# Gated mix of a spectral filter and a dense layer: the row transform in 32 half-width units, begun during the first matmul stage

## The chip, the cores and the metric

The kernel runs on one core of a Trainium2 chip. The metric is the device time of one execution in microseconds (us). Three runs of the kernel before gave 1273.38, 1273.94 and 1275.4 us; the median is 1273.94. The engines are named as in the profile: PE (TensorE, matrix products), PEld (its weight loads), DVE (VectorE), ACT (ScalarE), POOL (GpSimd) and SP (SyncE, which only issues transfers here). Each engine carries out its own instructions strictly in their order. ACT, POOL and SP also issue DMAs; such a line of the profile has a "q" behind the engine's name.

## The reference

For an input x of 2048 rows and 1024 columns, two branches are mixed by a gate for each row, and all gradients are taken for a given grad_out. It comes to nine outputs.

```python
def _A_ref(x, w_r, w_i):                    # spectral branch
    X = jnp.fft.rfft2(x.astype(jnp.float32), axes=(-2, -1))   # 2048 x 513, complex
    X = X * (w_r + 1j * w_i)
    return jnp.fft.irfft2(X, s=(S, D), axes=(-2, -1)).astype(jnp.bfloat16)

def _B_ref(x, w1, b1, w2, b2):              # dense branch, hidden width F = 3584
    h = jnp.einsum("bsd,df->bsf", x, w1) + b1
    r = jnp.where(h > 0, h, 0)
    return jnp.einsum("bsf,fd->bsd", r * r, w2) + b2

g = _sigmoid((x * gate_w).sum(-1, keepdims=True))
out = g * _A_ref(x, w_r, w_i) + (1 - g) * _B_ref(x, w1, b1, w2, b2)
# outputs: out, and its gradients for x, w_r, w_i, w1, b1, w2, b2, gate_w
```

The gradient of the spectral branch needs the same transform of the gated grad_out, so everything spectral is done for two arrays, called T = 0 (x) and T = 1 (the gradient).

## The kernel before, in words

**Two streams.** The main stream is the dense branch, in four stages one after another, all on TensorE in bf16:

- `mlp_in` (L671, 11 to 446 us): 112 units for the hidden layer (ph, L683) and 112 for its gradient (pd, L693), each of 8 matmuls of 128x512. A pair of them, 3.45 us, is counted as one unit here. ACT makes rT and h2T from ph, DVE makes dhT from pd, and both results go to DRAM. ph and pd share two banks of PSUM (the matmul accumulator memory). The weights w1g come in groups by SP, three buffers deep.
- `mlp_grads` (L785, 446 to 883 us): the gradients of w2 (pw, L824) and of w1 (pw, L840), 112 units of 16 matmuls, some 3.6 us each, into two banks. ACT evicts each unit (wo, L828 and L845). The left operand grp comes from DRAM by transposing DMAs on SP, two tiles in turn.
- `mlp_out` (L867, 883 to 1094 us; acc, L914), and then the gradient of x (`GradOfX.products`, 1094 to 1265 us; L1023).

The side stream is the spectral branch, as matmuls with small matrices of cosines and sines:

- The *first stages* (`first_stage_of_x`, `first_stage_of_grad`, L635 and L649) take 16 tiles for each T along the columns: fold (DVE), matmuls pk (L261), ACT copy ft, matmuls pu (`column_stage`, L294), copies and sums into u, store into the DRAM scratch z_scr by POOL (L283).
- `fft_mid` (L302) is the row transform. It runs over m = 0 to 15; each m covers a pair of row groups (n = 0, 1), 512 columns wide and for both T. For each m: load z (four DMAs) and the filter rows wn, sums pm (DVE), matmuls px with the matrices am (L378), ACT copies x (L380), products with the filter (DVE, L386 and L388), y (L395, L396), matmuls pv with bm (L414), ACT copy vc (L419), sums pc (DVE, L421 and L422), stores to y_scr (POOL, L438). The gradients of the filter are gs (DVE) and gw (ACT, L455, with buffers of two), stored by four DMAs (L461).
- The spectrum has 513 columns. Column 512 (the Nyquist column) and column 0 come by a way of their own: `edges` (L334) loads the edge columns of z_scr by nine small DMAs on SP into ed, low and mid, `edges_through` (L346) multiplies them with am (32 matmuls sp of 4 columns, L357) into ex, and DVE puts ex into columns 0 and 512 of x. On the way back, DVE gathers column 512 of y into ye, 32 matmuls si (L427) transform it, and DVE writes the outcome into column 0 of pc.
- `fft_out` (L506) takes 32 tiles. For each: load r from y_scr, issued by ACT (L521), DVE sums rf (L529, L530), matmuls pki (L537) on r and rf, ACT copy rt (L539), matmuls pui (L294), copies and sums, store to ax_scr. With the T = 0 tiles SP loads w2 in seven transfers of 1 MB.

**What sets the order.** Both streams are generators. `spread(main, side, per_main)` (L1146) runs main units and draws `per_main` side steps for each of them; the order that results, with the scheduler's own view of when operands are there, is the order of every engine. Before the change, in mlp_in 0.9 steps are drawn for a step of the main stream (72 of them, counted from where the transposes of the inputs are over), then the rest of the first stages follows at once, and beside the last units only the sums of the rows of dbn (the gradient of b2) run. `fft_mid` and half of `fft_out` are spread evenly over mlp_grads, some 1.6 steps for a unit; the other half of `fft_out` lies in mlp_out. The side stream has two 2-bank PSUM tiles in turn (tag "ps2"); small tiles (tag "tr") have a pool of their own, `tps`.

Of the kernel before, what the change touches and what calls it, by code (L numbers as in the profile page):

```python
# [10 lines left out]
P = 128  # L11
# [39 lines left out]
def build_consts(g: Geo):  # L51
# [54 lines left out]
    am, bm = np.zeros((P, R1 // 2, 2, P)), np.zeros((P, R1 // 2, 2, P))  # L106
    for m in range(R1 // 2):
        for n, k in enumerate(pair_of(m, R1)):
# [3 lines left out]
            bm[:, m, n] = np.block([[C_.T, S_.T], [-S_.T, C_.T]])  # L112
    c["am"] = (am * XS).astype(FDT_NP)
    c["bm"] = bm.astype(FDT_NP)
# [21 lines left out]
def kernel(  # L136
# [76 lines left out]
    z_scr = dram.tile([R1, R2, 2, 2, H], FDT, name="z_scr")  # L213
    y_scr = dram.tile([R1, R2, 2, 2, H], FDT, name="y_scr")
    rows_of = lambda scr, T: scr[:][:, :, :, T, :].rearrange("c (p i) x l -> i (c p) x l", i=S2)
# [52 lines left out]
    def first_columns(fb, cf, T, i, ft, earlier=None):  # L268
# [6 lines left out]
        uv = u[:].rearrange("p (c g i) -> p c g i", c=2, g=4)  # L275
        even = pu[:, 0, :].rearrange("p (h c i) -> p c h i", h=2, c=2)
        nc.scalar.copy(out=uv[:, 0, 0::2, :], in_=even[:, 0])
        nc.scalar.mul(out=uv[:, 1, 0::2, :], in_=even[:, 1], mul=flip[:])  # L278

        X, Y = (w[:, :, x] for x in range(2))  # L280
        V(out=uv[:, :, 1::2, 0 : P // 2], in0=X, in1=Y, op=ALU.add)
        V(out=uv[:, :, 3::-2, P - 1 : P // 2 - 1 : -1], in0=X, in1=Y, op=ALU.subtract)
        st(out=rows_of(z_scr, T)[i], in_=u[:].rearrange("p (x l) -> p x l", x=2))  # L283
# [18 lines left out]
    def fft_mid():  # L302
        fb, fbs = pool("f2", "right")
        NM, G = R1 // 2, nc.gpsimd
        lanes = [slice(R2 * n, R2 * (n + 1)) for n in range(2)]
        every = lambda w_, k: w_.rearrange("(q k) l -> k q l", k=R1)[k]
        am = fb.tile([P, NM, 2, P], FDT, name="am", tag="am")
        ld(out=am[:], in_=cten["am"].ap())
        bm = fb.tile([P, NM, 2, P], FDT, name="bm", tag="bm")
        ld(out=bm[:], in_=cten["bm"].ap())  # L310

        def inputs(m):
            z = fb.tile([P, 2, 2, H], FDT, name="z", tag="z", bufs=2)
            for n, c in enumerate((m, R1 // 2 + m)):
                for x in range(2):
                    ld(out=z[lanes[x], n], in_=z_scr[:][c, :, x ^ n if m else x])
            wn = fb.tile([P, 2, LW], BF16, name="wn", tag="wn", bufs=2)
            for c_, src_w in enumerate((A_w_r, A_w_i)):
                for n, k in enumerate(pair_of(m, R1)):
                    ld(out=wn[lanes[n], c_, 0:W1], in_=every(src_w, k))  # L320
            return z, wn
# [146 lines left out]
        for _ in range(3):  # L468
            yield
# [853 lines left out]
```

## Time and profile before

| what | value |
|---|---|
| median of three runs | 1273.94 us (1273.38 to 1275.4) |
| the profiled execution | 1274.6 us |
| its span, first to last instruction | 1272.8 us |
| mean granted clock of TensorE | 0.999 |
| busy in the span: PE, DVE, ACT, POOL | 1249.1, 706.4, 503.7, 270.9 us |
| instructions of PE, DVE, ACT, POOL in the trace | 6753, 1602, 793, 424 |
| moved by DMA | 233.27 MB, 183 GB/s in the mean |

The busy time of an engine is the time in which the profile shows it at work; issuing a DMA is not counted. The "40 slices" cut the span into 40 equal parts and give the busy share of each in tenths. A line of the groups names line, engine, operation, output and inputs with their sizes, the number of instructions, then busy time and the mean of one in ns, then idle time before them and what ended it. A line of the timeline has start, duration, engine, line, operation, output and inputs, and in brackets the idle time before it and what it waited for. A line of the waits has the total in us, the number of times and the longest.

### The profile page before, as it was taken

To read this page: it belongs to the slowest core of one execution; us is meant where nothing else is said; L and a number is where in the kernel's file an instruction comes from. 1 tells how busy PE (TensorE), PEld (TensorE's weight loads), DVE (VectorE), ACT (ScalarE), POOL (GpSimd) and SP (SyncE) were. 2 spreads that over 40 slices of the span, in tenths; PEclk is the share of its full clock that TensorE was granted. 3 is DMA by queue.
4 is the path that set the end of the run, shared out by engine and by line. 5 is a ranking of instruction groups with operands and counts; after the bars stand their busy time and mean duration, and the time that the engine had idled before them with its cause. 6 is when DMAs were issued, how large, how long until landed. Compare 5 with 4: busy or idle time off the path is not lost.

```text
span 1272.8 us, 18282 instructions
## 1 busy us (share of the span) xinstructions
PE 1249.1 (98%) x6753; PEld 609.6 (48%) x6884; DVE 706.4 (56%) x1602; ACT 503.7 (40%) x793; POOL 270.9 (21%) x424
## 2 busy tenths in 40 slices
PE   8999999999999999999999999999999999999997
PEld 5555544555544444444444444555445454444443
DVE  3554433445481216676756661343867767896573
ACT  4656654666633334554555552443112111010100
POOL 0111111111110124445545542222010101000000
PEclk9999999999999999999999999999999999999999
DMA  9566353646353879998898678994999898565530
GB/s 287 199 186 186 134 157 117 182 140 183 112 153 70 196 194 201 259 244 193 194 193 201 133 161 230 305 244 164 229 225 221 192 212 203 153 190 174 169 113 34
DMA packets 326260, 233.27 MB, mean 183 GB/s; under 512 B 195308, under 2 KB 279434, under 8 KB 325914
## 3 DMA queue, kind: packets, MB, share of 16 engines
q1 hardware_dynamic: 291120, 141.19, 48.4%
q0 software_dynamic: 26144, 82.47, 19.1%
q10 hardware_dynamic: 8906, 8.43, 2.3%
q8 instruction: 54, 0.88, 0.3%
q14 instruction: 36, 0.29, 0.1%
HBM read 106.19 MB, written 81.81 MB: 148 GB/s over the span
## 4 chain that ended last, share of the span: by engine, by line
PE 61%; DVE 4%; DMA 2%; issue 2%; ACT 1%; POOL 0%; SPq 0%; ACTq 0%; DVEq 0%; POOLq 0%
PE acc L914 14%; PE pw L824 13%; PE pw L840 12%; PE xX L1023 7%; PE xV L1023 3%; PE pd L693 3%; PE ph L683 3%; PE xZ L1023 2%; PE pui L294 1%; PE pki L537 1%; PE px L378 1%; PE pv L414 1%; DMA r<-y_scr 1%; DMA out_dram<-wo 1%; ACT x L380 1%
## 5 line engine op out<-in xcount | busy, mean ns | idle before, releaser
L683 PE MATMUL ph<-xT,w1g 128*128 128x512 bf16 x864 | 216.9, 379 | 2.7 <-DMA w1g<-in_B_w_dram 1.2
L693 PE MATMUL pd<-dbT,w2T 128*128 128x512 bf16 x877 | 209.8, 379 | 1.6 <-DVE dhT L697 0.4
L840 PE MATMUL pw<-grp,res 128*128 128x512 bf16 x872 | 198.8, 379 | 2.3 <-ACT wo L845 1.1
L824 PE MATMUL pw<-dbn,grp 128*128 128x512 bf16 x876 | 198.9, 379 | 1.9 <-ACT wo L828 0.7
L914 PE MATMUL acc<-w,hblk 128*128 128x512 bf16 x873 | 196.5, 379 | 1.2
L697 DVE SCALAR_TENSOR_TENSOR dhT<-pd,rT 128x512 bf16<-128x512 f32 x112 | 77.3, 691 | 202.9 <-PE pd L693 159.7
L824 PEld LDWEIGHTS <-grp 128*128 128x128 bf16 x896 | 87.0, 98 | 104.6 <-issue 1.5
L693 PEld LDWEIGHTS <-w2T 128*128 128x128 bf16 x896 | 87.0, 98 | 103.5 <-issue 1.2
L840 PEld LDWEIGHTS <-res 128*128 128x128 bf16 x896 | 86.1, 98 | 99.8 <-issue 1.4
L914 PEld LDWEIGHTS <-hblk 128*128 128x128 bf16 x896 | 86.4, 98 | 97.9
L683 PEld LDWEIGHTS <-w1g 128*128 128x128 bf16 x896 | 84.5, 98 | 90.5 <-DMA w1g<-in_B_w_dram 1.5
L685 ACT ACTIVATE rT<-ph,b1col 128x512 bf16<-128x512 f32 x112 | 77.0, 687 | 116.7 <-PE ph L683 113.1
L982 ACT ACTIVATE g<-gatew_bc,dsc 128x1024 f32<-128x1024 bf16 x16 | 18.3, 1148 | 146.8 <-DVE gxo L1032 120.6
L845 ACT CAST wo<-pw 128x512 bf16<-128x512 f32 x56 | 32.6, 585 | 106.3 <-PE pw L840 57.1
L686 ACT ACTIVATE h2T<-rT 128x512 bf16<-128x512 bf16 x112 | 70.5, 630 | 2.5
L539 ACT CAST rt<-pki 128x1024 f16<-128x1024 f32 x32 | 32.5, 1015 | 95.0 <-PE pki L537 92.9
L1023 PEld LDWEIGHTS <-dS 128*128 128x128 f16 x448 | 43.7, 98 | 53.3 <-DVE dS L1011 0.5
L828 ACT CAST wo<-pw 128x512 bf16<-128x512 f32 x56 | 32.6, 583 | 87.5 <-PE pw L824 58.6
L380 ACT CAST x<-px 64x1024 f16<-64x1024 f32 x64 | 64.4, 1007 | 0.7
L283 POOL DMA_DIRECT2D z_scr<-u x32 | 23.2, 726 | 171.2 <-ACT u L278 101.4
L738 POOL DMA_DIRECT2D h2T_scr<-h2T x28 | 20.4, 727 | 183.0 <-ACT h2T L686 167.4
L566 POOL DMA_DIRECT2D ax_scr<-yo x32 | 17.3, 540 | 167.9 <-DVE yo L565 126.2
(189 smaller groups left out, 1610.6 us busy)
## 6 DMA issues: line engine op xcount, KB each, us to landing
h2T_scr<-h2T POOLq DMA_DIRECT2D x28, 512.0 KB, 4.3
dhT_scr<-dhT POOLq DMA_DIRECT2D x28, 512.0 KB, 4.6
hblk<-h2T_scr SPq DMA_DIRECT2D x16, 896.0 KB, 7.6
hblk<-dhT_scr SPq DMA_DIRECT2D x16, 896.0 KB, 8.7
z_scr<-u POOLq DMA_DIRECT2D x32, 256.0 KB, 3.1
z<-z_scr SPq DMA_DIRECT2D x64, 128.0 KB, 3.5
y_scr<-pc POOLq DMA_DIRECT2D x64, 128.0 KB, 4.3
r<-y_scr ACTq DMA_DIRECT2D x32, 256.0 KB, 4.3
```

The costliest lines, as they stand in the source:

```text
L380: nc.scalar.copy(out=x[lanes[n], c, :, 0:H], in_=px[lanes[c]])
L683: mm(ph[:], lhsT=w1g[:, dc, fc % 2 * P : (fc % 2 + 1) * P], rhs=xT[:, dc, ss], start=(dc == 0), stop=(dc == DC - 1))
L685: nc.scalar.activation(rT[:], ph[:], ACT.Relu, bias=b1col[:, fc : fc + 1])
L686: nc.scalar.activation(h2T, rT[:], ACT.Square)
L693: mm(pd[:], lhsT=w_[:, ec, fc % FGC * P : (fc % FGC + 1) * P], rhs=dbT[:, ec, ss], start=(ec == 0), stop=(ec == DC - 1),)
L697: return STT(out=dhT, in0=pd[:], scalar=2.0, in1=rT[:], op0=ALU.mult, op1=ALU.mult, accum_out=gb1part[:, fc, sb : sb + 1],)
L824: mm(pw[:], lhsT=cur[:, t, fb_ * P : (fb_ + 1) * P], rhs=dbn[:, t, hf * H : (hf + 1) * H], start=(t == 0), stop=(t == NT - 1),)
L828: last = nc.scalar.copy(out=wo[:, hf * H : (hf + 1) * H], in_=pw[:])
L840: mm(pw[:], lhsT=xr[t][:, d_ * P : (d_ + 1) * P], rhs=cur[:, t, :], start=(t == 0), stop=(t == NT - 1),)
L845: nc.scalar.copy(out=wo[:], in_=pw[:])
L914: turn["PE"] = mm(acc[:], lhsT=cur[:, fc, t2 * P : (t2 + 1) * P], rhs=w2[:, fc, cs], start=(fc == 0), stop=(fc == FC - 1))
L1023: mm(acc[:], lhsT=lhs[:, fc, :], rhs=rhs[:, fc, :], start=start and fc == 0, stop=fc == KH - 1, skip_group_check=True,)
```

## The change

`fft_mid` is done in 32 units instead of 16: for each m first the upper half of the columns (h = 1), then the lower (h = 0), each 256 wide. All tiles of a unit (z, pm, x, t, y, pc, gs) have half the width, and both n and both T of a unit go through one PSUM tile. The scratch arrays z_scr and y_scr get the layout (row group, row, real/imaginary, h, T, column), so that a z load or a y store of a unit is one DMA for each n; a row tile (the u stores, by POOL; the r loads, by ACT) now takes three DMAs instead of one. In fft_out ACT copies the even columns of r into a tile re, from which the matmuls read.

The Nyquist column is packed: its filtered value (eh, from the h = 1 unit) is added to or subtracted from column 0 of the products in the h = 0 unit. The si matmuls, ye and the repairs of pc disappear. For this the rows of the matrices are interleaved anew (ab, one load of 128 KB for each m, in place of am and bm); am is loaded in two halves for the edges alone, into a buffer of the products. The edge columns take twelve DMAs instead of nine. gs, gw and pm have one buffer instead of two; gw is written in two halves and stored once for each m. ACT instead of DVE puts ex into x.

The side stream is one generator (first stages, sums of db, fft_mid, fft_out), drawn at 1.25 steps for a unit through all of mlp_in. 9 of the 32 units of fft_mid begin there, the others run beside mlp_grads. fft_out keeps its place to within two units, and mlp_out and the gradient of x keep their order. When the transposes of the inputs are over, `tps` is closed and ph/pd get four banks instead of two; sp and other small tiles move to "ps2". To make room, w1g has two buffers instead of three, the tiles h2T and dhT three instead of four, and of the two tiles for grp one lies in a pool opened with mlp_grads.

```diff
+    def rows_of(issue, scr, T, i, sb, stored):
+        far = scr[:].rearrange("c (p i) x h t l -> i t (c p) x h l", i=S2)[i, T]
+        near = sb[:].rearrange("p (x h l) -> p x h l", x=2, h=2)
+        lo, hi = slice(0, P // 2), slice(P // 2, P)
+        pairs = [(far[lo], near[lo])] + [(far[hi][:, 1 - x], near[hi][:, x]) for x in range(2)]
+        for a, b in pairs:
+            issue(out=a, in_=b) if stored else issue(out=b, in_=a)
...
+        def edges():
...
+            for x in range(2):
+                for t in range(2):
+                    e = 2 * x + t
+                    ld(out=ed[lanes[0], :, 0, e], in_=col[:, 0:NM, x, t])
+                    ld(out=low[lanes[1], :, e], in_=col[:, NM:, 1 - x, t])
+                    ld(out=mid[lanes[0], e : e + 1], in_=col[:, NM, 1 - x, t : t + 1])
...
+            sp = fps.tile([P, NM, 2, 4], FP32, name="sp", tag="ps2", bufs=2)
+            for h in range(2):
...
+                if h == 0:
+                    am = some_am(1)
+                    for _ in range(4):
+                        yield
...
+        def transform(m, h, pm, ex):
+            x = fb.tile([P, 2, 2, WL], FDT, name="x", tag="x", bufs=2)
+            px = fps.tile([P, 2, 2, HW], FP32, name="px", tag="ps2", bufs=2)
+            for n in range(2):
+                mm(px[:, n], lhsT=mats[m][:, 0, n, :], rhs=pm[:, n], start=True, stop=True)
+            for n in range(2):
+                for c in range(2):
+                    nc.scalar.copy(out=x[lanes[n], c, :, 0:HW], in_=px[lanes[c], n])
+            nc.scalar.copy(out=x[:, :, :, h * HW], in_=ex[:, m, :, :, h])
+            return x
...
+        def back(m, h, y):
...
+            for n in (1, 0):
+                mm(pv[:, n], lhsT=mats[m][:, 1, n, :], rhs=y[:, n], start=True, stop=True)
...
+                vc = fb.tile([P, 2, HW], FP32, name="vc", tag="vc")
+                nc.scalar.copy(out=vc[:], in_=pv[:, 1])
+                V(out=pc[:, 0], in0=pv[:, 0], in1=vc[:], op=ALU.add)
+                V(out=pc[:, 1], in0=pv[:, 0], in1=vc[:], op=ALU.subtract)
+            for n, c in enumerate((m, R1 // 2 + m)):
+                st(out=y_scr[:][c, :, :, h].rearrange("r x t l -> (r x) t l"), in_=pc[:, n])
...
+        def grads_out(m, h, gs, gw):
+            nc.scalar.mul(
+                out=gw[:, :, h * HW : (h + 1) * HW].rearrange("p c (i g) -> p c i g", g=4),
+                in_=gs[:, :, 0:HW].rearrange("p c (g i) -> p c i g", g=4), mul=GS,
+            )
+            nc.scalar.mul(out=gw[:, :, h * H], in_=gs[:, :, h * HW], mul=0.5 * GS)
+            if h == 0:
...
+        turns = [(m, h) for m in range(NM) for h in (1, 0)]
...
+        for u, (m, h) in enumerate(turns):
+            if h:
+                eh = fb.tile([P, 2, 2, 2], FDT, name="eh", tag="eh")
+            x = transform(m, h, pm, ex)
             yield
             if held:
+                back(*turns[u - 1], held)
+            tt = products(h, x, w)
+            yield
+            if u:
+                grads_out(*turns[u - 1], gs, gw)
+            held = joined(h, tt, eh)
+            yield
+            gs = grads_of_w(h, x)
...
     def fft_out():
...
-            nc.scalar.dma_start(out=r[n][:].rearrange("p (x l) -> p x l", x=2), in_=rows_of(y_scr, T)[i])
+            rows_of(nc.scalar.dma_start, y_scr, T, i, r[n], False)
...
+            evens[n] = fb.tile([P, 2, 2, P], FDT, name="re", tag="re", bufs=2)
+            for im in range(2):
+                nc.scalar.copy(
+                    out=evens[n][:, im].rearrange("p g (h i) -> p g h i", h=2),
+                    in_=rv[:, im, :, 0::2, :].rearrange("p h g i -> p g h i"),
+                )
...
     def mlp_in():
+        banks, drawn = [mps], [0]
+
+        def bank(name):
+            drawn[0] += 1
+            return banks[drawn[0] // 2 % len(banks)].tile([P, SW], FP32, name=name, tag="ph", bufs=2)
+
+        def more_banks():
+            tps_s.close()
+            more, mores = pool("mps1b", "left", PSUM)
+            banks.append(more)
+            mpss.callback(mores.close)
...
-            w1[fp] = wb.tile([P, DC, PW], BF16, name="w1g", tag="w1g", bufs=3)
+            w1[fp] = wb.tile([P, DC, PW], BF16, name="w1g", tag="w1g", bufs=2)
...
-    first = firsts()
-    n = 0
-    mixed = spread(units, first, 0.9)
-    while n < 72:
-        next(mixed)
-        n += 1
-    for _ in first:
-        pass
...
+    def aside():
         yield from stage
         yield from first_stage_of_grad()
...
+        yield from sums_of_db()
         yield from fft_mid()
         yield from fft_out()
 
...
+    for _ in spread(units, spec, 1.25):
+        pass
+    grads = mlp_grads()
     next(grads), next(grads)
-    todo = 13 + 6 * (R1 // 2) + 2 * NT
+    todo = 22 + 2 * (NT + 4) + NT + 1 + 9 + 4 * R1 + 1 + 4 + 2 * NT - count[0]
     for _ in spread(grads, spec, todo / (2.0 * FG * FGC * NH - 2)):
         pass
```

## The prediction, made before the changed kernel was run

> **What bounds the kernel now.** I read four views in this order: the busy times, the 40 slices, the waits of TensorE, and then windows of 40 us, because the question is only where TensorE is not full. The page first:
>
> ```profile
> PE 1249.1 (98%) x6753; PEld 609.6 (48%) x6884; DVE 706.4 (56%) x1602; ACT 503.7 (40%) x793; POOL 270.9 (21%) x424
> ...
> PE   8999999999999999999999999999999999999997
> ...
> ACT  4656654666633334554555552443112111010100
> ...
> PEclk9999999999999999999999999999999999999999
> ```
>
> TensorE is busy for 98% of the span, in every slice but the first and the last, at an undisturbed clock. So engine time elsewhere is free as long as it makes TensorE wait for nothing, and a change can win only what matmuls it removes and what idle time it closes. How much idle time there is inside is read from the windows (length, then busy time of PE, weight load, DVE, ACT, POOL, clock, DMA share, GB/s):
>
> ```profile
> 320.00:360.00 40.00, 39.73 (x228) 20.15 (x232) 21.24 (x55) 24.02 (x46) 5.81 (x8) 1.00 0.49 133
> 360.00:400.00 40.00, 39.42 (x179) 17.77 (x182) 22.88 (x37) 14.55 (x23) 4.36 (x6) 1.00 0.25 92
> ...
> 480.00:520.00 40.00, 39.79 (x184) 18.17 (x187) 25.91 (x46) 20.17 (x23) 18.32 (x26) 1.00 1.04 216
> ...
> 600.00:640.00 40.00, 39.15 (x184) 17.89 (x186) 25.23 (x45) 23.06 (x25) 20.11 (x31) 1.00 0.95 180
> 640.00:680.00 40.00, 38.90 (x181) 17.66 (x184) 25.51 (x47) 21.37 (x24) 18.77 (x29) 1.00 1.02 213
> 680.00:720.00 40.00, 39.20 (x183) 17.89 (x186) 27.49 (x47) 20.31 (x24) 21.60 (x33) 1.00 0.63 151
> ...
> 760.00:800.00 40.00, 38.55 (x204) 18.29 (x207) 11.82 (x35) 11.67 (x19) 12.80 (x24) 1.00 0.91 238
> ```
>
> A full window shows 39.79. Against it the row transform (fft_mid, 450 to 770 us) loses 0.64 + 0.89 + 0.59 = 2.1 us in three windows, its passage into fft_out 1.24 us, and the passage from the first stages to the sums of db 0.37 us (360 to 400). The idle time is really a little longer than shown: an isolated 512-column matmul is written down as 379 ns, while in a row of them one starts every 216 ns, so each stop hides 0.16 us. With that I count 2.8, 2.0 and 0.8 us. That is nearly all the change can touch. The waits and one place in the timeline tell what kind they are:
>
> ```profile
> PE pw L840 <- ACT wo L845: 1.1, 2, 0.6
> PE pv L414 <- ACT x L380: 0.9, 2, 0.6
> PE pw L824 <- ACT wo L828: 0.7, 1, 0.7
> ```
>
> ```profile
> 630.76 2.00 ACT L455 ACTIVATE gw<-gs 128x1024 bf16<-128x1024 f16 x1 [4.39 <-DVE gs L454]
> 632.40 0.19 PE L427 MATMUL si<-ye,bm 128*128 128x4 f16 x2
> 632.67 1.05 ACT L828 CAST wo<-pw 128x512 bf16<-128x512 f32 x2
> 633.29 3.61 PE L824 MATMUL pw<-dbn,grp 128*128 128x512 bf16 x16 [0.69 <-ACT wo L828]
> ```
>
> The eviction wo, which frees a bank for the next 3.6 us of matmuls, stood behind one 2.0 us ScalarE instruction (gw), and TensorE stopped. Long instructions on ScalarE's in-order queue are the cause inside fft_mid.
>
> **The change part by part.** The sum is made against the profiled execution: 1272.8 us of span and 1.8 us around it, 1274.6, which is 0.66 above the median of the runs shown, 1273.94.
>
> *Matmuls removed.* The 32 si matmuls go. They are listed at 166 ns, but the 32 sp matmuls (same shape) ran back to back in 0.95 us. I take 32 x 0.03 = 0.9 us gained; the other end is 16 pairs at the 0.19 us shown, 3.1. All other matmuls keep their columns, only split differently.
>
> *Pieces half as long.* px copies go from 64x1024 at 1.007 us to 64x512 (the 128x512 wo costs 0.59), gw from one of 1.98 us per m to two of about half, vc (1.02) and the pc sums (1.22) likewise. The queue ahead of wo gets shorter, and a unit of half the work comes every 3.25 main units (12 us; 24 us per m) where a whole m came every 4.6 (17 us). The three windows' idle time can go wholly; I take all 2.8 us, ends 0 and 2.8. What is late next at such a place is wo itself, 0.59 us after pw, which two banks cover.
>
> *Four banks and continuous side work in mlp_in.* The side stream (first stages, sums of db, then 9 of the 32 fft_mid units) runs at 1.25 steps per main unit to the end of mlp_in, where before it ran at 0.9 and then only sums. The ph/pd tiles get four banks instead of two, so the stop at 371 us (0.8 with the hidden part) should be covered: 0.8 gained, ends 0 and 0.8. Against it, the denser first stages put a pu block after its own pk with five 0.216 us matmuls between, 1.08 us, where the copy ft takes 1.01: a few stops of 0.1 to 0.2 us, +0.3 (0 to 3).
>
> *Edges.* In the changed order the first sp matmul is unit 83 of 112. The loads of its edge columns stand on SP behind the w1g load, whose buffer is now one of two and comes free when unit 79 ends. That leaves about 3.5 units at 3.45 us, 12.1 us. Behind it SP issues w1g, am and twelve edge loads:
>
> ```profile
> 457.57 0.63 SPq L341 DMA_DIRECT2D ed<-z_scr  x1
> ...
> 466.67 0.67 SPq L343 DMA_DIRECT2D mid<-z_scr  x1
> 470.06 0.16 DVE L348 COPY ed<-mid 64x4 f16<-64x4 f16 x1
> ...
> 478.58 0.95 PE L357 MATMUL sp<-ed,am 128*128 128x4 f16 x32
> ```
>
> One issue is 0.63 to 0.67 us and the last one lands 3.4 us later. 0.9 + 12 x 0.65 + 3.4 + 1 for the DVE pieces is 13.1; up to 16 if the issues meet as many gaps as the nine here (9.1 us from first to last). So TensorE waits 1 to 4 us, unless the scheduler's place for w1g lets SP start earlier; I take +1.5, ends 0 and 4. Queued behind that wait are the ph/pd units, nothing else hides it. The second half of am is loaded over the first and has three units, 10 us, against the 5.5 in which the whole am landed: nothing.
>
> *Second grp tile.* It now lies in memory that mlp_in gives up, so its four transposes (3.4 to 3.9 us each on SP, 6.4 to landing) start at the end of mlp_in: 22 us against the 8 units of the first group, 29 us. Nothing; with 7 us less cover it would be late.
>
> *Passage to fft_out.* The chain is shorter: half a vc, pc at 0.69 instead of 1.22, two y_scr stores instead of four, no si. But an r tile is now three DMAs, and all are issued by ScalarE, ahead of wo:
>
> ```profile
> 778.77 0.97 ACTq L521 DMA_DIRECT2D r<-y_scr  x2
> 779.86 0.59 ACT L845 CAST wo<-pw 128x512 bf16<-128x512 f32 x1 [6.11 <-DMA out_dram<-wo]
> 780.50 3.61 PE L840 MATMUL pw<-grp,res 128*128 128x512 bf16 x15 [0.51 <-ACT wo L845]
> 784.45 0.29 DVE L529 TENSOR_TENSOR rf<-r 128x256 f16<-128x256 f16 x1 [12.03 <-DMA r<-y_scr]
> ```
>
> Six issues of 0.37 us instead of two are +1.5; shorter chain -1.9. New is that ScalarE itself copies the even columns (re<-r) and so waits for r, where only DVE and TensorE waited before. I take -0.4 (-1.9 to +5.4, worked out under the rivals).
>
> *Hidden work.* ScalarE gets some 290 more instructions: 64 re copies (0.42 us, by the DVE copy of that size), 64 more issues (23 us), 32 ex copies, each px copy's fixed part; about 55 us. In 450 to 760 us it is busy 155 of 310 us and in 80 to 350 us 164 of 270, so it is covered. POOL's 64 more z_scr issues (0.53 to 0.73 us) come on 271 of 1273 us, SP's 19 instructions on an idle queue, DVE's pieces at 56%. Single gs, gw and pm buffers: a gw store lands in 4.0 us in the median, one m lasts 24 us; +0.3 (0 to 4, for a chain gs, gw, store that runs late beside 1 MB loads). If that cover went, ScalarE would hold back wo and the price would be the excess over one unit, 3.6 us.
>
> One rule speaks against the split. The Trainium skill, "DMA: Bandwidth & Descriptors", "Anatomy of one DMA", puts a fixed part of about 2.0 us on each DMA, and by it 128 more transfers would be 256 us of latency, ruinous if any were in series. This case's trace agrees on the size: 64 KB gw stores land in 4.0 us, 256 KB r loads in 4.3. They overlap here, so my sum holds only the issue times. By the rule alone the passage would cost two more fixed parts, 4 us, and the forecast would be no change.
>
> A second one is "Double-buffer for performance" in "Trainium Kernel Development and Optimization", "Best Practices", which the single gw and gs buffers go against. No row of before shows them single.
>
> *Sum:* -0.9 - 2.8 - 0.8 + 0.3 + 1.5 - 0.4 + 0.3 = -2.8. 1274.6 becomes 1271.8 in a profiled run, 1271.1 in the median.
>
> **The rivals.** 0.2%, 2.55 us, is about what a measurement here tells from no change.
>
> *No change.* The edge wait at 4 us and a stop or two of fft_mid surviving (half of 2.8 gained): -0.9 - 1.4 - 0.8 + 0.3 + 4 - 0.4 + 0.3 = +1.1, so 1275.0; with only one of them, 1272.5 to 1273.6. For it speaks the SP arithmetic above; against it, the w1g load may be issued earlier.
>
> *Slower: ScalarE caught at the passage.* It stands in order: r issues that wait until y_scr has landed, wo, re copies that wait until r has landed, wo. An r load landed 4.8 to 9.6 us after its issue beside the seven 1 MB w2 loads (12.7 us in the median). At 9.6, ScalarE is held about 9.6 - 1.5 - 0.6 = 7.5 us, of which one unit of pw covers 3.6: 3.9 us of idle TensorE, with the 1.5 of issues +5.4 instead of -0.4. That gives +3.0, 1276.9, and a second such tile 1280.8. It decides from about 9 us of landing on. Against it: the third tile's load was already 4 us ahead in the trace, and later ones longer.
>
> *The stops don't go.* If they come from DMA landing and not from long ScalarE pieces, only si and the bank gain remain: 1273.9. The line at 630.76 speaks against it; this goes with no change.
>
> **How the numbers follow.** Forecast 0.44 (faster 0.40, same 0.04, as 1271.1 lies near the bound of 1271.4); no change 0.25; ScalarE caught 0.31 (slower, 0.01 of it same). The range goes from 1266.0 (si at 3.1, passage -1.9, no edge wait: -8.6 at most, little chance below) to 1281.0, two caught tiles. The forecast's own range is 1267.0 to 1273.0. Sum of the cases: faster 0.40, same 0.30, slower 0.30.
>
> **What would show it.** Right: 32 matmuls fewer than 6753; the windows between 480 and 760 us at 39.6 to 39.8; PE waits for wo gone; a wait of sp for an ed copy near unit 83 (370 to 390 us) of 1 to 2 us. The passage, around 770 to 790 us, decides: a re copy that waits for r with wo behind it and PE pw waiting for wo is the slower rival. Wrong in another way: waits of PE for ft or u in 60 to 350 us (the denser first stages), or ScalarE waiting for gw's store.

## The result, and the profile after

The changed kernel takes 1304.09 us (median; 1302.24 to 1305.32) against 1274.67 for the kernel before beside it: a ratio of 1.023, 95% interval 1.0212 to 1.0248. It is slower by 29 us, where the forecast had been 1271.1 and the range ended at 1281. The profiled execution took 1302.24 us with a span of 1300.5.

The page of the changed kernel, the busy times, TensorE's slices and the granted clock:

```profile
span 1300.5 us, 18819 instructions
...
PE 1259.0 (97%) x6722; PEld 610.4 (47%) x6852; DVE 719.4 (55%) x1742; ACT 536.6 (41%) x1016; POOL 313.8 (24%) x520
...
PE   9999999999899979999999998899999999999998
...
PEclk9999999999999989999999998899999999999999
```

Two things differ from before. TensorE has weak slices around 340, 470 and 780 to 845 us, and the clock row is lower in the last two of these places; the windows below show it lower in the first and around 660 us too. Of the 27.7 us by which the span grew, 17.8 are more idle time (41.5 against 23.7) and 9.9 are more busy time, although 32 matmuls are gone (the weight loads, of which every one is recorded, fell from 6884 to 6852). The end of the kernel hides a part of the loss. The last instruction of VectorE, before and after, is

```profile
1265.11 0.69 DVE L1032 TENSOR_TENSOR gxo<-xV,g 128x512 bf16<-128x512 f32 x1 [2.33 <-PE xV L1023]
```

```profile
1295.76 0.69 DVE L1064 TENSOR_TENSOR gxo<-xV,g 128x512 bf16<-128x512 f32 x1 [2.33 <-PE xV L1055]
```

so the work ends 30.7 us later, and the rest of the span behind it (the last store and the closing instructions, called the tail below) is 4.0 us instead of 7.0. The windows in which the time is lost (columns as before):

```profile
320.00:360.00 40.00, 35.61 (x172) 16.05 (x174) 7.46 (x27) 13.16 (x20) 8.05 (x12) 0.96 0.55 138
440.00:480.00 40.00, 32.32 (x144) 14.21 (x146) 25.04 (x66) 22.49 (x42) 15.79 (x26) 0.96 0.72 165
640.00:680.00 40.00, 37.72 (x166) 16.72 (x167) 20.31 (x48) 17.44 (x35) 15.42 (x25) 0.96 0.70 151
760.00:800.00 40.00, 36.10 (x163) 16.21 (x165) 9.55 (x23) 11.05 (x21) 9.69 (x18) 0.96 0.66 176
800.00:840.00 40.00, 33.89 (x183) 16.74 (x187) 10.17 (x43) 17.11 (x34) 6.49 (x12) 0.87 1.07 275
```

No engine is near full in them, so it is not work that was too much but waits. (The DMA share is over 1 in the last window, but it was 1.13 in the same window of the kernel before, with TensorE full.) The waits of TensorE, and of ScalarE before gw:

```profile
PE pw L871 <- ACT wo L876: 9.5, 3, 3.9
PE pw L855 <- ACT wo L859: 8.6, 3, 6.0
PE sp L355 <- DVE ed L350: 4.1, 1, 4.1
PE pd L724 <- DVE dhT L728: 1.7, 3, 0.9
```

```profile
ACT gw L466 <- DMA out_dram<-gw: 25.7, 4, 8.2
```

A few long stops make up nearly all of it. Each has a place in the timeline. First the edges:

```profile
334.54 0.37 SPq L746 DMA_DIRECT2D w1g<-in_B_w_dram  x1
...
337.32 2.92 SPq L334 DMA_DIRECT2D mid<-z_scr  x1
...
350.66 0.68 PE L355 MATMUL sp<-ed,am 128*128 128x4 f16 x16 [4.07 <-DVE ed L350]
```

SP issued w1g at 334.5, needed 13 us for am and the twelve edge loads (one tiny mid load held it 2.9 us), and TensorE stood 4.1 us before sp. Then gw:

```profile
469.08 1.09 POOL L474 DMA_DIRECT2D out_dram<-gw  x2
...
478.36 1.06 ACT L466 ACTIVATE gw<-gs 128x512 bf16<-128x512 f16 x1 [8.16 <-DMA out_dram<-gw]
...
479.43 1.05 ACT L859 CAST wo<-pw 128x512 bf16<-128x512 f32 x2
480.04 1.44 PE L855 MATMUL pw<-dbn,grp 128*128 128x512 bf16 x3 [6.00 <-ACT wo L859]
...
481.70 4.65 PE L855 MATMUL pw<-dbn,grp 128*128 128x512 bf16 x16 [0.22 <-issue]
```

With one gw buffer the next gw waits until the four stores of the last have landed, 8.2 us, and the two evictions wo stand behind it on ScalarE. The last line is the slow clock: 16 matmuls take 4.65 us instead of 3.61 after the stop, the later ones at full speed again. And the passage to fft_out:

```profile
788.45 4.14 ACTq L227 DMA_DIRECT2D r<-y_scr  x6
...
792.70 0.58 ACT L876 CAST wo<-pw 128x512 bf16<-128x512 f32 x1 [8.47 <-DMA r<-y_scr]
793.34 5.30 PE L871 MATMUL pw<-grp,res 128*128 128x512 bf16 x15 [2.82 <-ACT wo L876]
...
800.93 0.40 ACT L542 COPY re<-r 128x256 f16<-128x256 f16 x1 [2.95 <-DMA r<-y_scr]
...
801.87 8.42 PE L871 MATMUL pw<-grp,res 128*128 128x512 bf16 x31 [2.79 <-ACT wo L876]
...
820.86 5.35 ACTq L227 DMA_DIRECT2D r<-y_scr  x3
...
826.94 4.00 PE L871 MATMUL pw<-grp,res 128*128 128x512 bf16 x9 [3.86 <-ACT wo L876]
```

There are three stops there, in turn behind six r issues that waited for y_scr and then took 4.1 us, behind re, which waited for r, and behind three r issues. The last line of these, `x3`, runs from the start of the first issue to the end of the third, so it holds the waits between them: a single r issue takes 0.62 us in the median (0.58 to 1.06 over all 96). The chain that ended last between 808 and 829 us tells what the second issue waited for:

```profile
810.96 13.98 DMA grp<-dhT_scr
824.95 0.02 issue
824.97 0.58 ACTq L227
```

It began when a transpose of grp, issued by SP at 810.96, had landed. r has nothing to do with grp; what the two share is a semaphore. In the trace the DMAs of ScalarE and of SP signal with the same eight semaphores and those of GpSimd with eight others, and a held issue begins when the transfer that used its semaphore last has landed (here number 117).

### The profile page after: what moved, and what is told of

It is laid out like the page before. It is cut to its first block, busy times and chain, and to the rows that moved or that the text cites. A ratio compares the mean times of both kernels' runs of the same rounds, so it can differ in the third digit from the quotient of the medians.

```text
span 1300.5 us, 18819 instructions
## 1 busy us (share of the span) xinstructions
PE 1259.0 (97%) x6722; PEld 610.4 (47%) x6852; DVE 719.4 (55%) x1742; ACT 536.6 (41%) x1016; POOL 313.8 (24%) x520
## 4 chain that ended last, share of the span: by engine, by line
PE 73%; DMA 6%; DVE 5%; issue 4%; ACT 2%; POOL 2%; SPq 1%; ACTq 0%; POOLq 0%; DVEq 0%
PE acc L946 14%; PE pw L855 11%; PE pw L871 11%; PE ph L714 10%; PE pd L724 10%; PE xX L1055 7%; PE xV L1055 3%; DMA out_dram<-gw 3%; PE xZ L1055 2%; PE pu L307 1%; PE pui L307 1%; DMA grp<-dhT_scr 1%; PE pki L555 1%; PE pk L274 1%; ACT x L414 1%
## 5 line engine op out<-in xcount | busy, mean ns | idle before, releaser
L871 PE MATMUL pw<-grp,res 128*128 128x512 bf16 x873 | 203.7, 386 | 10.9 <-ACT wo L876 9.5
L871 PEld LDWEIGHTS <-res 128*128 128x128 bf16 x896 | 88.0, 99 | 114.0 <-issue 17.5
L466 ACT ACTIVATE gw<-gs 128x512 bf16<-128x512 f16 x32 | 34.9, 1090 | 137.9 <-DVE gs L462 112.2
L227 POOL DMA_DIRECT2D z_scr<-u x96 | 59.0, 620 | 115.2 <-ACT u L291 58.1
L1014 ACT ACTIVATE g<-gatew_bc,dsc 128x1024 f32<-128x1024 bf16 x16 | 18.3, 1148 | 146.8 <-DVE gxo L1064 120.5
L414 ACT CAST x<-px 64x512 f16<-64x512 f32 x128 | 74.1, 579 | 3.1 <-PE px L411 1.9
L876 ACT CAST wo<-pw 128x512 bf16<-128x512 f32 x56 | 32.5, 583 | 86.6 <-PE pw L871 40.1
L403 DVE TENSOR_TENSOR pm<-z 128x512 f16<-128x512 f16 x30 | 12.7, 424 | 89.4 <-PE px L411 89.4
L584 POOL DMA_DIRECT2D ax_scr<-yo x32 | 17.4, 542 | 168.9 <-DVE yo L583 126.5
L877 POOL DMA_DIRECT2D out_dram<-wo x56 | 30.9, 552 | 98.7 <-ACT wo L876 86.8
```

The costliest lines, as they stand in the source:

```text
L227: issue(out=a, in_=b) if stored else issue(out=b, in_=a)
L414: nc.scalar.copy(out=x[lanes[n], c, :, 0:HW], in_=px[lanes[c], n])
L466: nc.scalar.mul(out=gw[:, :, h * HW : (h + 1) * HW].rearrange("p c (i g) -> p c i g", g=4), in_=gs[:, :, 0:HW].rearrange("p c (g i) -> p c ...
L871: mm(pw[:], lhsT=xr[t][:, d_ * P : (d_ + 1) * P], rhs=cur[:, t, :], start=(t == 0), stop=(t == NT - 1),)
```

## The experiments

Theory A: the time is lost at these places, each by ScalarE (or the edge loads) holding TensorE, and each has its own price, its stop and the slow clock behind it. Theory B: the denser order has no room, and a stop that is taken away comes back elsewhere. The others are named where they come up. "Over" is the difference of the median from that of the kernel before on the same chip; the changed kernel is 29.4 over.

**Two gw buffers.**

```diff
-                gw = fb.tile([P, 2, LW], BF16, name="gw", tag="gw")
+                gw = fb.tile([P, 2, LW], BF16, name="gw", tag="gw", bufs=2)
```

> The changed kernel with two gw buffers again; the order of instructions on every engine is the same. Theory A (four separate places where ScalarE or the edge loads hold TensorE, each with its own price): the stops of 6.0 us at 474 and 2.0 us at 665, where ScalarE waited for the store of gw to land, go, and with them the slow clock behind them (1.6 and 1.0 us): 1304.1 - 11 = 1293, between 1292 and 1296. Theory B (the denser work has no room, a stop that is taken away comes back at the next operand): TensorE stops at the same places for gs or pm instead, over 1300.

1291.63 us, 18.1 over (ratio 1.0144, 1.0129 to 1.0159): 11.3 us gained; the profile shows the slowest execution, 1294.27. ScalarE's wait for gw's store is gone from its waits, and so are the stops of TensorE for dhT, so these came from the same hold. One stop of 3.0 us stayed at the old place, with another releaser:

```profile
474.55 1.06 ACT L466 ACTIVATE gw<-gs 128x512 bf16<-128x512 f16 x1 [5.19 <-DVE gs L462]
...
476.23 1.01 PE L855 MATMUL pw<-dbn,grp 128*128 128x512 bf16 x2 [3.02 <-ACT wo L859]
```

gw now waits for gs, which VectorE brings late, and wo stands behind it as before. So the price held, and in one place Theory B is right too.

**Edges later.**

```diff
         z = {0: inputs(*turns[0])}
-        for _ in range(4):
+        for _ in range(10):
...
-    todo = 22 + 2 * (NT + 4) + NT + 1 + 9 + 4 * R1 + 1 + 4 + 2 * NT - count[0]
+    todo = 22 + 2 * (NT + 4) + NT + 1 + 15 + 4 * R1 + 1 + 4 + 2 * NT - count[0]
```

> The changed kernel with six more empty side steps between the edge loads and the matmuls sp, so sp comes some five units (17 us) later. Theory A: the stop of 4.1 us before sp and 1.0 us of slow clock behind it go, everything behind is only shifted: 1304.1 - 5 = 1299, 1297 to 1301. Theory B: the wait is for a transfer that comes later with sp, or fft_mid, begun later, crowds the rest: 1303 or more.

1287.30 us, 13.8 over (1.0106, 1.0084 to 1.0128): 15.6 us gained, three times what was expected; the profile shows the slowest execution, 1290.68. The wait before sp fell from 4.1 to 0.5 us, as Theory A had it; but the later start also moved fft_mid against the stores and transposes, and ScalarE's wait for gw's store came down to

```profile
ACT gw L466 <- DMA out_dram<-gw: 13.4, 2, 8.5
```

So what one gw buffer costs depends on where a store falls beside other transfers, and this run doesn't price the edges alone.

**re on VectorE.**

```diff
-                nc.scalar.copy(
+                nc.vector.tensor_copy(
                     out=evens[n][:, im].rearrange("p g (h i) -> p g h i", h=2),
```

> The changed kernel with the copies re<-r on VectorE instead of ScalarE; TensorE's order is the same. Theory A, part one (ScalarE waiting in re for r to land, with wo behind it): the stop of 2.8 us at 799 with 0.7 of slow clock goes, the one at 823 (3.9 and 1.4), which stands behind r issues, shrinks or stays: 1304.1 - 3.5 = 1300.6, 1297 to 1301. Theory C (only the issues of r on ScalarE count): no change, 1303 to 1305.

1309.94 us, 36.4 over (1.0284, 1.0268 to 1.0299): 6 to 7 us slower still, a miss of both theories. But most of it does not come from the edit. TensorE's order is the same in both profiles, so its weight loads can be compared one by one: they are 6.5 us later already at 775 us, before fft_out begins (2.7 of it in the first 20 us, the rest at sp and inside fft_mid), and 8.1 us later at 860. What differed there is not known; the passage itself cost 1.6 us more. It has the clearest case of a held issue:

```profile
823.29 10.49 ACTq L227 DMA_DIRECT2D r<-y_scr  x3
...
833.90 0.58 ACT L876 CAST wo<-pw 128x512 bf16<-128x512 f32 x1 [10.11 <-issue]
```

The chain through it, between 817 and 836 us:

```profile
817.88 14.63 DMA grp<-dhT_scr
832.51 0.02 issue
832.53 0.60 ACTq L227
...
833.17 0.62 ACTq L227
...
833.90 0.59 ACT wo L876
...
834.54 1.86 PE pw L871 x4
```

Three issues of 0.6 us each held ScalarE for 10.5 us, because the second waited 8.6 us for the transpose of grp that had its semaphore. SP had four transposes under way from 817.9 to 836.9.

**r loads by GpSimd.**

```diff
-            rows_of(nc.scalar.dma_start, y_scr, T, i, r[n], False)
+            rows_of(nc.gpsimd.dma_start, y_scr, T, i, r[n], False)
```

> The changed kernel with the r loads issued by GpSimd instead of ScalarE, re still on ScalarE. Theory C (issues): the stops at 790 (2.8, wo behind six issues that wait for y_scr) and at 823 (3.9, wo behind three issues of 1.8 us each) go with 2 us of slow clock: 1304.1 - 9 = 1295, 1293 to 1298. Theory A, part one (the wait in re): they come back in re, as r lands no earlier: 1301 to 1304.

1303.51 us, 30.0 over (1.0236, 1.0201 to 1.0271): no gain in the time, which is what Theory A had said. In the profile (1302.03) both theories have a part: r lands no earlier, and TensorE waited 5.0 us for re, but by its weight loads it made up 5.6 us at the passage. It had come there 4.2 us late, from longer stops behind gw, which the edit doesn't touch (11.1 us against 8.6 behind wo), and the tail is 1.1 us longer. The distance between the last y_scr store and the first pki is the same as before; the next run lengthens it.

**A longer passage.**

```diff
-        load(0), load(1)
-        for _ in range(4):
+        for _ in range(4):
+            yield
+        load(0), load(1)
+        for _ in range(8):
             yield
...
-    todo = 22 + 2 * (NT + 4) + NT + 1 + 9 + 4 * R1 + 1 + 4 + 2 * NT - count[0]
+    todo = 22 + 2 * (NT + 4) + NT + 1 + 9 + 4 * R1 + 1 + 12 + 2 * NT - count[0]
```

> The changed kernel with more distance at the passage to fft_out: four empty side steps between the last y_scr store and the first r loads, and eight instead of four from there to the first fold. The r issues then find y_scr landed and re finds r landed. Theory A: the three stops of 2.8 to 3.9 us between 790 and 830 and their slow clock (12.7 us together) go: 1291, 1288 to 1298, as fft_mid gets a little denser (a unit every 3 main units) with its single gw buffer. Theory D (ScalarE has not the time for 3 issues of 0.65 us and two copies per tile, whatever the distance): stops of 2 to 4 us appear later among the pw units, 1300 or more.

1296.64 us, 22.8 over (1.0182, 1.0157 to 1.0207): 6.6 us gained where 12.7 were expected. At the passage one stop of 4.0 us behind wo and one of 1.0 remained of 9.5, while ScalarE's wait for gw's store rose to 46.9 us in eight places (25.7 in four), with a longest stop of TensorE of 7.2. That fft_mid had got denser may be a reason, but it is not shown: the fourth run, at the old density, has 37.9 us in six places.

**The kernel before with one gw buffer.**

```diff
-            gw = fb.tile([P, 2, LW], BF16, name="gw", tag="gw", bufs=2)
+            gw = fb.tile([P, 2, LW], BF16, name="gw", tag="gw", bufs=1)
```

> The kernel before with one gw buffer instead of two, nothing else. Theory A (the single buffer hurts because a new m's first half follows 12 us after the last half of the old one, while the stores land up to 9 us after their issue, and issue comes late): here the next gw comes 17 us later, so no change, 1272 to 1276. Theory E (one buffer is too few at any pace, since a store waits behind the transposes of grp): several stops of 2 us or more with slow clock, 1280 or more.

1274.04 us, ratio 1.0004 (0.9994 to 1.0013): no difference. At 17 us from one gw to the next, in whole pieces, the second buffer is worth nothing; what costs is one buffer at the changed pace.

**All three: two gw buffers, later edges, longer passage** (the edits above).

> The changed kernel with all three: two gw buffers, six more empty steps before sp, the longer passage. Theory A with additive prices: 1304.1 - 11 - 5 - 12.7 = 1275, and a stop or two of ScalarE waiting for gs (3 us with one buffer taken away in the first run) may stay: 1272 to 1280. If the stops of fft_mid are really gone, as the full windows between 520 and 760 us say, it ends at the forecast of 1271. Theory B (stops come back elsewhere): 1283 or more.

1278.15 us, 4.4 over (1.0038, 1.0025 to 1.0051): 25 of the 29 us are accounted for. The single gains measured above, 11.3, 15.6 and 6.6, add up to 33.5; they are not additive, since each of the first two takes away stops behind gw. From 480 us on fft_mid is without a stop; its windows in this profile, in which every matmul is recorded and a full one shows 40.00:

```profile
480.00:520.00 40.00, 40.00 (x187) 18.06 (x186) 23.98 (x56) 21.10 (x41) 15.99 (x26) 1.00 0.70 166
...
640.00:680.00 40.00, 40.00 (x187) 18.14 (x186) 25.64 (x58) 18.89 (x38) 18.30 (x30) 1.00 0.93 207
```

What stays is 1.6 us for gs at 461 and two stops at the passage, 2.9 us before pw (wo) and 3.4 us before pui (e). In both, r issues of ScalarE had waited for transposes of grp, until 765.44 and until 802.93 us.

**The same with the r loads by GpSimd.**

> The seventh run's kernel (two gw buffers, later sp, longer passage) with the r loads issued by GpSimd instead of ScalarE; TensorE's order is the same. Theory F (with enough distance, what is left at the passage is ScalarE held in its own r issues, which take up to 2.2 us each while SP's transposes or 1 MB loads are under way): the stops of 2.9 us at 764 and 3.4 us at 802 go with their slow clock, 1278.2 - 7.5 = 1270.7, 1269 to 1273. Theory G (ScalarE waits for r to land, whoever issues it): the stops come back before re, 1276 to 1280.

1274.20 us, ratio 1.0002 (0.9993 to 1.0011): 4 us gained, about half of what was expected. GpSimd's DMAs do not share a semaphore with SP's, and no r issue waits for a transpose any more. The stop of 3.4 us went; the one at 764 stayed with 3.6 us, now behind four re copies that waited for r. So each theory is right at one stop, except that what held ScalarE was the wait in front of the issues, not their length. The transposes of grp became slower: the four from 787 us took 29.4 us, against 18.3 in the seventh run.

**Only the longer passage and GpSimd.**

> The changed kernel with the longer passage and the r loads by GpSimd, one gw buffer and the early sp kept. Theory F: against the run with the longer passage alone (1296.6) the stop of 4.0 us at 779 and its slow clock go, 1291, 1288 to 1294; the stops at gw and sp stay. Theory G: 1295 to 1298.

1302.58 us, 28.8 over (1.0215, 1.0196 to 1.0235), with executions from 1298.92 to 1306.71, of which the profile shows the slowest: a miss of both. The passage was better (4.0 us in three stops), but a new one came at 845, 6.6 us for grp, and gw stayed at 6.7. SP's transposes took from 810.4 to 852.2 for five, more than 8 us each.

**The kernel before with its r loads in three pieces.**

```diff
-            nc.scalar.dma_start(out=r[n][:].rearrange("p (x l) -> p x l", x=2), in_=rows_of(y_scr, T)[i])
+            near, far = r[n][:].rearrange("p (x l) -> p x l", x=2), rows_of(y_scr, T)[i]
+            nc.scalar.dma_start(out=near[: P // 2], in_=far[: P // 2])
+            for x in range(2):
+                nc.scalar.dma_start(out=near[P // 2 :, x], in_=far[P // 2 :, x])
```

> The kernel before with each r load cut into three DMAs on ScalarE as in the changed kernel (one half of the partitions in one, the other in two), nothing else. Theory F: ScalarE issues six instead of two before the first wo of the passage, +1.5 to +3 us there and 0.7 to 1.3 us more per tile, hidden elsewhere: 1275 to 1279. If three issues cost nothing in an order without re: 1273 to 1275. If the issues themselves are the whole price of the passage in the changed kernel: 1283 or more.

1281.67 us, 7.9 over (1.0061, 1.0048 to 1.0074): more than expected. With no re, no new layout and nothing else moved, three issues in place of one put ScalarE's hold into the kernel before. In the kernel before no r issue waited for a semaphore in use; here four did, 10.8 us together, 7.1 of them for a transpose of grp (the issue at 812.10) and 1.8 for a load of w2 (the next):

```profile
812.10 2.70 ACTq L524 DMA_DIRECT2D r<-y_scr  x2
814.92 0.58 ACT L848 CAST wo<-pw 128x512 bf16<-128x512 f32 x1 [9.96 <-DMA w<-in_B_w_dram]
...
815.56 1.01 PE L843 MATMUL pw<-grp,res 128*128 128x512 bf16 x2 [5.86 <-ACT wo L848]
```

**All three, GpSimd and re on VectorE.**

> The eighth run's kernel (two gw buffers, later sp, longer passage, r loads by GpSimd) with re on VectorE as well, so that ScalarE neither issues r nor waits for it; TensorE's order is the same. Theory A: the last stop of the passage (3.6 us before pw at 764, wo behind re) goes with its slow clock, 1274.2 - 4.5 = 1269.7, 1268.5 to 1271.5, faster than before and near the forecast. Theory G: TensorE itself waits for r before pki, or wo for something else, 1273 to 1275.

1280.21 us, 6.1 over (1.0042, 1.003 to 1.0055), a miss. ScalarE holds nothing at the passage any more, and the next operand is late:

```profile
PE pw L873 <- DMA grp<-dhT_scr: 8.1, 2, 6.4
```

SP issued the seven 1 MB loads of w2 (11.4 us) just ahead of the transposes of grp, and eight transposes then took 50.2 us, 6.3 each; in the kernel before four took 17.5 us at this place. The w2 loads alone do not explain it: in the seventh run they stood ahead of the transposes in the same way, and four took 18.3 us.

**That kernel with sp at its early place** (four empty steps again).

> The same kernel with sp at its place in the changed kernel (four instead of ten empty steps after the edge loads). Theory A with its price for the edges alone: one stop of 3.7 to 4.2 us before sp and 1.0 us of slow clock, + 5 on the run beside it, 1274.7 (1273 to 1276.5). If the second run's gain of 17 us was mostly the edges, + 10 or more; if it was only the other phase of fft_mid, + 0 to 2.

1292.59 us, 18.4 over (1.0148, 1.0133 to 1.0163), but the profile is of its fastest execution, 1282.71 us, and the four others lay between 1292.2 and 1294.5. In the profile sp waits 4.2 us, gw's lateness for gs is back (3.0 us), 3.6 us are lost behind wo at the passage, and nothing is lost for grp. What the slower executions wait for was not seen, so the edges' price in an otherwise mended kernel stays open.

**The eleventh kernel with w2 loaded by GpSimd.**

```diff
-                    ld(out=w2[:, fc : fc + 4, :], in_=B_w2[fc * P : (fc + 4) * P, :].rearrange("(q p) e -> p q e", p=P))
+                    nc.gpsimd.dma_start(out=w2[:, fc : fc + 4, :], in_=B_w2[fc * P : (fc + 4) * P, :].rearrange("(q p) e -> p q e", p=P))
```

> The eleventh run's kernel with the seven 1 MB loads of w2 issued by GpSimd instead of SP; TensorE's order is the same. Theory H (the stops of 1.8 and 6.4 us at 816 and 818, where TensorE waits for grp, come from SP issuing the transposes of grp behind the w2 loads): they go, 1280.2 - 9 = 1271, 1269 to 1273. Theory I (the transposes themselves run slower, 6.3 instead of 3.9 us each, beside the r loads in pieces of 512 B and w2, whoever issues them): grp stays late, 1276 to 1284.

1273.45 us, ratio 0.999 (0.9975 to 1.0005), with executions from 1267.37 to 1276.77. The profile shows the fastest:

```profile
span 1265.6 us, 18956 instructions
...
PE 1254.3 (99%) x6852; PEld 608.3 (48%) x6852; DVE 727.2 (57%) x1806; ACT 518.9 (41%) x952; POOL 378.7 (30%) x623
```

Of the stops behind wo, sp and grp only the 1.6 us behind gw at 461 are left. The time is 6.5 us under the 1273.84 beside it, but only about half of that is the change. The work ends with

```profile
1261.68 0.69 DVE L1066 TENSOR_TENSOR gxo<-xV,g 128x512 bf16<-128x512 f32 x1 [2.33 <-PE xV L1057]
```

3.4 us before that of the kernel before in its profile, and the tail is 3.2 us instead of 7.0. So 3.4 us, between these two profiles, is what the change with these edits does when no transfer is late. Moving w2 didn't bring the transposes back to their old length (27.1 us for the four from 782 us, against 36.6 in the eleventh run and 17.4 in the kernel before), but with them TensorE didn't wait in this execution.

**The kernel before with the r loads by GpSimd.**

```diff
-            nc.scalar.dma_start(out=r[n][:].rearrange("p (x l) -> p x l", x=2), in_=rows_of(y_scr, T)[i])
+            nc.gpsimd.dma_start(out=r[n][:].rearrange("p (x l) -> p x l", x=2), in_=rows_of(y_scr, T)[i])
```

> The kernel before with its r loads issued by GpSimd instead of ScalarE, nothing else. Theory F: two or three stops of the passage there (2.0 us together) have ScalarE's issue waiting for y_scr ahead of wo, and go: 1272.0, 1271 to 1273. If TensorE then waits for r in pki instead: 1273 to 1275.

1270.83 us, ratio 0.998 (0.9971 to 0.9988): faster than both kernels, with one word changed, but not for the reason that Theory F gives. In the profile (1271.88) the passage is worse: one stop behind wo went, and in place of it TensorE waits for r,

```profile
786.18 0.40 PE L537 MATMUL pki<-ki,r 128*128 128x128 f16 x4 [2.52 <-DMA r<-y_scr]
```

The work then ends with

```profile
1266.08 0.69 DVE L1032 TENSOR_TENSOR gxo<-xV,g 128x512 bf16<-128x512 f32 x1 [2.33 <-PE xV L1023]
```

1.0 us later than in the profile of the kernel before (1265.11). The span is 2.7 us shorter all the same, as the tail is 3.3 us instead of 7.0. So the gain seen in these profiles lies wholly behind the work, and the run doesn't show that the move helps the passage.

**The thirteenth kernel, twice more.**

> The thirteenth run's kernel again, one look: its executions lay between 1267.4 and 1276.8 and the profile shows the fastest. If the spread is landing times of DMAs, a slower execution shows one or two stops of 2 to 7 us with a wait for a transfer (r, grp or the store of gw), at a place where the fast one has none; if it is only the clock, no stop and a lower granted clock.

> The same once more, a second look, with the same two answers.

1269.81 and 1272.52 us. Both show a stop before pw at 817 that the fastest execution doesn't have, 1.6 and 3.5 us, both for grp; the times are 2.4 and 5.2 us above the fastest. So the spread, as far as it was seen, is mostly the landing of one transposed tile, with its slow clock in the second case. The four transposes from 782 us took 30.8 and 31.6 us there, against 27.1 in the fastest execution.

## Why the prediction was wrong, point by point

**Passage, -0.4 (-1.9 to +5.4).** The rival "ScalarE caught at the passage" is what happened in its first two holds: r issues behind y_scr and re behind r. They stopped TensorE for 2.8 us each, together close to the +5.4 of one caught tile. The third hold, 3.9 us, is in neither the sum nor the rival. The step that failed is "six issues of 0.37 us instead of two are +1.5": it priced an issue by its own length and put its wait at nothing. A piece takes 0.62 us to issue, which would have been a small error; but with three issues for a tile an issue of ScalarE can find its semaphore still with a transfer of SP, and waits until that has landed, with wo behind it. In the kernel before that never happened to an r load. The tenth run, in which only the r loads are cut, prices it at 7.9 us, and the traces of the changed kernel and of six other runs show an r issue that begins as a transpose of grp with its semaphore lands. That the eight semaphores come round sooner with three issues than with one is the likely reason, but only argued. In all, 9.5 us of stops were measured at the passage, some 15 with the slow clock (an estimate: TensorE worked 3.4, 2.7 and 4.8 us at half clock there).

The Trainium skill's fixed part for each DMA ("DMA: Bandwidth & Descriptors", "Anatomy of one DMA") is stated there for DMAs that GpSimd issues, and counts until they have landed. "Agrees on the size" was too kind: the 64 KB gw stores landed in 4.0 us before and 5.3 after, twice the page's 2.0 and more, and r pieces, which ScalarE issues, in 4.5 and 6.2 us in the changed kernel, against 4.3 for the whole tile. So later landing showed too, but no run separates it from the waits of the issues.

**Single buffers, +0.3 (0 to 4).** I held the 4.0 us in which a store lands in the median against the 24 us of an m. The right pair is the late store against the free time: gw is written in two halves, so between the second half of one m and the first of the next lies one unit, 12 us, of which the store's issue behind other work on GpSimd and a landing of 8.5 us took all. The prediction named the chain (gs, gw, store) and its price, the excess over one unit; it gave one case where four came. Two buffers gave back 11.3 us. The sentence of the Trainium skill ("Trainium Kernel Development and Optimization", "Best Practices": double-buffer) was on the right side in the changed kernel; in the kernel before a second gw buffer was worth nothing (ratio 1.0004). In these two kernels the measured pace decided, not the rule.

**Edges.** The mechanism and the arithmetic were right, 1 to 4 us; the 1.5 taken was too kind. 4.1 us of wait were measured. From the issue of w1g to sp it was 16.1 us, the upper end, because single mid loads held SP for up to 2.9 us. No run prices this stop alone.

**A price that was missing: the clock behind a stop.** Every price in the sum was the idle time. In the changed kernel the granted clock stood at half in six stretches of 3.4 or 6.8 us, one at or behind each of six stops; two of them:

```profile
477.00:483.80 6.80, 3.54 (x8) 1.28 (x9) 0.00 (x0) 2.12 (x4) 0.61 (x1) 0.50 1.03 286
...
825.20:832.00 6.80, 4.84 (x12) 1.73 (x13) 2.64 (x11) 3.57 (x7) 1.62 (x3) 0.50 1.27 278
```

TensorE was busy for 21.0 us in the six, so at full clock it would have needed some 10.5 us less (an estimate from these rows). It agrees with the 9.9 us of added busy time, and with 1265.3 us of it in the first run (mean clock 0.991) against 1254.3 in the thirteenth (1.0), with the same 6852 matmuls recorded.

**What came true.** The 32 si matmuls were worth 0.9 to 1.5 us: with all records there, TensorE's busy time is 1255.2 us in the kernel before with one gw buffer, 1255.8 in it with r by GpSimd, and 1254.3 in the thirteenth run, at clocks of 0.999 and 1.0. The stops inside fft_mid do go, once ScalarE isn't held otherwise, and the one at 371 us went with the four banks or the moved sums (360 to 400 us is full at 39.79). ScalarE's and GpSimd's added work was covered, VectorE's but for the 1.6 us in which gs is late at 461. The forecast's gains were some 4.5 us; in the fastest execution of the mended kernel the work ends 3.4 us earlier, with these 1.6 us against it. So the gains were real, and the waits that the change itself brings outweigh them several times.

**Denser first stages, +0.3.** Right in size: from 40 to 320 us TensorE shows 277.4 us of work, 277.9 before, and no wait for ft or u is among its waits.

**The low end of the range.** 1266.0 is 8.6 under the profiled 1274.6; by the median, as the other figures are given, it would have been 1265.3. Nothing hangs on it here.

## What to carry to other kernels

At 98% on one engine, look at what stands ahead of its evictions on every in-order queue, and ask of each instruction there whether it waits for a transfer: a buffer made single, a copy that reads a fresh load, or a DMA issue that must first get its semaphore back from another queue's transfer can each hold the main stream for a landing time, and a landing has to be priced late, not at its median. Cutting one load into three cost more here than the added issue time: in the tenth run it brought such waits where there had been none. Read a merged line of issues (`x3`) one by one before calling the issue slow. Giving such issues to GpSimd freed ScalarE in the eighth run (4 us), but a later operand can use the gain up, as grp did in the ninth and eleventh. And when a time changes, see first at which matmul the profiles part: it was before the edited place in the third run, and behind all the work in the fourteenth.

## What the hardware showed that was not expected

- The issues of r by ScalarE are of nearly constant length, 0.62 us in the median in pieces and 0.37 whole; what made three of them last 5.35 or 10.49 us is a wait for a transfer of SP with the same semaphore. Issued by GpSimd they took 0.6 us each throughout, without such waits.
- The clock at half came in stretches of 3.4 us or two or three times that, mostly at stops of 2 us and more. The length of a stop alone doesn't decide it: the 3.0 us before pw in the first run had it (0.89 in the mean from 470 to 485 us), the 3.0 us at the same place in the twelfth had not (1.00), and neither had the 2.5 us in the fourteenth.
- The transposes of grp slow down where r comes in pieces issued by GpSimd: the slowest four of a grp tile took 25 to 37 us in those runs, 14 to 20 with the pieces issued by ScalarE, 15 to 22 with whole tiles by either. Why is open.
- The tail behind the last work goes with the number of GpSimd instructions in the trace: 7.0 us in the three kernels with 424, 3.3 with 456, 4.0 to 4.1 in six with 520, 5.1 in five with 616 and 3.2 in three runs with 623. In the kernel before, 3.7 us of it lie between the last instruction of SP and the next of GpSimd. Why is open too; differences of a few us between kernels are not to be read without it.
